# Eleven, nine and eight: where the 64-bit cosine weights are converted in an attention, experts and cosine-FFN kernel

## The chip, the cores and the metric

The kernel runs on one core of one Trainium2 chip. The time is the device time of one execution in microseconds (us). The engines of the core have names in the profile: PE is the matrix engine (PEld is its weight load), DVE the vector engine, ACT the scalar engine, POOL the GpSimd engine, and SP the engine whose queue issues nearly all DMAs here.

## The reference

```python
x = _attn_ref(q, k, v)            # 4 batches, 8 heads, 576 tokens, window 128 -> 2304 x 512
# experts: 8 of them, D = 512, F = 1024, tokens weighed by a Sinkhorn-normalised gate P
h = np.maximum(x @ w1[e], 0.0)
out += P[:, e:e + 1] * (h @ w2[e])
# cosine FFN: w_in 512 x 2048, w_out 2048 x 512, both float64 on the way in
h = x @ w_in
g = h * np.cos(h)
return (g @ w_out).astype(np.float32)
```

The two FFN weights come as 64-bit floats. The kernel reads them as pairs of 32-bit integers and makes 32-bit floats out of them on the chip.

## The kernel before

After the attention (about the first 195 us), the 2304 tokens are handled in three blocks of 768, first three expert blocks ("moe" 0, 1 and 2), then three FFN blocks. A block of experts is 32 units (8 experts, 4 slices of 256 hidden columns each, `u` from 0 to 31), an FFN block is 8 units. Each product of a unit is done with seven half-size products (a Strassen scheme, `m` in the order 5, 1, 4, 2, 3, 6, 7), and each operand is split into a high and a low part, so that one such product is six matmuls. All instructions are issued in an order that the program writes out by hand; each engine works through its own list in that order and waits where an operand isn't ready.

In block 0 a unit is the seven first-layer products (`product`, L938) and, between m = 6 and m = 7, `batch()`: six token tiles of the second layer (`g2`, L1163 to L1165), each followed by `evac` on DVE (L1154), with three PSUM banks gT[0..2] in turn. Beside it block 0 prepares its expert weights: `prep_a` splits the first-layer weights of the next unit (L142 on ACT, L145 on DVE: three instructions, the last one of 1024 columns), `prep_s` makes sums on POOL (L132), `prep_b` and `prep_sb` do the same for the second layer (L159, L184 on ACT, L161, L181 on POOL, L186 on DVE). The first product of a unit (m = 5, bank z) takes its weights from the part that the last L145 writes: `unit_mm` issues for each half high-high, high-low and low-high, so the third matmul of the product is the first to read the low part.

In blocks 1 and 2 the split weights are read back from DRAM (`load_a`, L115), the second layer runs as Strassen products too (`s_step`, L1077 on PE, evacuated by L1089 on DVE, operands from L1097 on DVE, L1101 on ACT, L1110 on POOL, weights by L1105 on SP's queue), and `load_p` brings a row of gate weights (L878).

Small work is woven in by generators. `slot()` steps the first one of each of the lists `pre`, `sbq`, `feed`, `bg` and `bg2` by one yield. In block 0 a unit calls it ten times: after the products 5, 1, 4, 2 and 7, and in `batch()` after each of the tiles 1 to 5, where `step_all(pre)` follows once more. In blocks 1 and 2 there are twelve calls in a unit. `bg` holds first the late gates, the Sinkhorn iterations and `p_rows` (its last act is the DMA at L866), and then `convert_f64`.

`convert_f64(c)` converts one chunk of 128 x 512 values. There are 32 chunks. Its steps, one for each call of `slot()`: DVE L260, ACT L264, nothing, DVE L267, DVE L271, DVE L275, DVE L279, the load of the next chunk (`load_f64`, L245 or L251 on SP's queue, 512 KB), nothing, the store of the result (L287, 256 KB). Four chunks are converted during the attention. When the chunks of an FFN unit are done, `prep_ffn` (in `bg2`) splits them: four sums on POOL (L132), eleven copies on ACT (L220), eleven differences on POOL (L222) and eleven stores (L216).

The lines that append a conversion are in the main loop, at the end of a unit:

```python
if chunk < 4 * NU2 and not bg and kind == "moe" and (b == 1 and u < NU1 - 6 or b == 2 and 0 < u < NU1 - 8) and u % 8 in (0, 2, 3, 5, 7):
    bg.append(convert_f64(chunk))
    chunk += 1
if b and ready < NU2 and 4 * (ready + 1) <= chunk - 1 + (not bg) and not bg2:
    bg2.append(prep_ffn(NU1 + ready))
    ready += 1
```

Of the kernel before, what the change touches and what calls it, by code (L numbers as in the profile page):

```python
# [29 lines left out]
def tile_attention_moe_cos_ffn(ctx, tc, q, k, v, w_gate, w1, w2, w_in, w_out, out):  # L30
# [9 lines left out]
    NU1 = E * UPE  # L40
    NU2 = DFF // FU
# [30 lines left out]
    with tc.manual_schedule():  # L72
# [38 lines left out]
        def load_a(u, ms):  # L111
            o = sorted(WI[m] for m in ms)
            o = slice(o[0], o[-1] + 1, o[-1] - o[0] or 1)
            out = waX[:, u % 2].bitcast(F32).rearrange("p (o w) -> p o w", o=7)
            nc.sync.dma_start(out=out[:, o], in_=wd1[u].rearrange("p (o w) -> p o w", o=7)[:, o])  # L115
# [187 lines left out]
        def stages(b, src):  # L303
            b11, b12, b21, b22 = quarters(b, src)
            st = {}
            stg[b] = st

            def stage(nm, i, x, y, over=None):
                if over:
                    t = st[over]  # L310
                elif b[0] == "ffn":
                    t = rawp.tile([P, 4, P, 2], F32, tag=("ra", "rb")[i], name=f"st{nm}_{b[0]}{b[1]}")
                    t = t.rearrange("p a f c -> p (a f c)")[:, :TB].rearrange("p (k f) -> p k f", k=2)
                else:
                    t = u_pool.tile([P, 2, HB], F32, tag=("u1", "u2")[i], name=f"st{nm}_{b[0]}{b[1]}")
                t = like(b, t) if not over else t
                nc.gpsimd.tensor_tensor(out=t, in0=x, in1=y, op=ALU.subtract)
                st[nm] = t

            stage("T1", 0, b12, b11)  # L320
            yield
            yield
            stage("T2", 1, b22, st["T1"])
            yield
            if b[0] == "ffn":
                yield
                stage("T3", 0, b22, b12)
                yield
                yield
                stage("T4", 1, b21, st["T2"])  # L330
                yield
            else:
                st["after"] = {"T2": lambda: stage("T4", 1, b21, st["T2"], "T2"),
                               "T1": lambda: stage("T3", 0, b22, b12, "T1")}
# [28 lines left out]
        def gate_block(j, pool, sb):  # L363
            b, o = j // 2, j % 2 * HB
            ps = pool[0].tile([P, 512], F32, tag=pool[1], name=f"gate{j}")
            for kc in range(KC):
                nc.tensor.matmul(ps[32 * kc:32 * kc + 32, :HB], wg[:, kc, :], xr[b][:, kc, o:o + HB],
                                 tile_position=(0, 32 * kc), skip_group_check=True)
            lT = sb if isinstance(sb, bass.AP) else sb.tile([P, HB], F32, tag="lT", name=f"lT{j}")
            nc.scalar.activation(out=lT, in_=ps[:, :HB], func=AF.Copy)  # L370
            return lT

        def gate_block2(j, lT, pool):
            ps = pool[0].tile([P, 512], F32, tag=pool[1], name=f"gateT{j}")
            for tt in range(GPB):
                nc.tensor.matmul(ps[:, tt * E:(tt + 1) * E], lT[:, tt * P:(tt + 1) * P], sel)
            nc.vector.tensor_copy(
                logits[:, j * GPB:(j + 1) * GPB, :].rearrange("p t e -> p (t e)"), ps[:, :GPB * E]
            )
# [334 lines left out]
        chunk = []  # L714
# [122 lines left out]
        bg, bg2, pre, feed, sbq = [], [], [], [], []  # L837

        def step_all(lst):
            if lst and next(lst[0], StopIteration) is StopIteration:  # L840
                lst.pop(0)

        def lazy(f):
            yield from f()
# [28 lines left out]
        def load_p(g):  # L873
            b, e = divmod(g, E)
            if b >= NB - 1:
                return
            src = pT.rearrange("(i e) t -> e i t", e=E)[e, b * TPB:(b + 1) * TPB, :]
            nc.sync.dma_start(out=Pb(g).rearrange("p (i t) -> p i t", t=P), in_=src.partition_broadcast(P))  # L878
# [335 lines left out]
        def tick():  # L1214
            tail[:] = [t for t in tail if next(t, StopIteration) is not StopIteration]

        def late_gates():
            bank_ = (LastBank(), "m")
            for j in range(next_half, 2 * NB):
                o = (1 + 2 * (j % 2)) * TB  # L1220
                lT = gate_block(j, bank_, cX[:, o:o + HB])
                yield
                yield
                gate_block2(j, lT, bank_)

        bg.append(late_gates())
        bg.append(sinkhorn((LastBank(), "m"), skp))
        bg.append(p_rows())
# [3 lines left out]
        chunk, ready = n_f64[0], 0  # L1232
# [17 lines left out]
        for n, s in enumerate(steps):  # L1250
            kind, b, u = s
            pre += pre_next
            pre_next.clear()
            ph = phases.index((kind, b))
            last = n + 1 == len(steps) or steps[n + 1][:2] != (kind, b)
            nxt = phases[ph + 1] if ph + 1 < len(phases) else None
            to_end = (NU1 if kind == "moe" else NU1 + NU2) - u
            if nxt and to_end == 4:
                if nxt[0] == "ffn":
                    feed.append(lazy(lambda nxt=nxt: stages(nxt, accs["moe", nxt[1]])))  # L1260
                else:
                    feed.append(stages(nxt, xr[nxt[1]]))
            if (kind, b, u) == ("moe", 1, 0):
                load_p(0)
            pace = NEXT if nx else {}
            if last and nxt:
                while feed:
                    step_all(feed)
                pace = LAST
                nx = combos(nxt, xr[nxt[1]] if nxt[0] == "moe" else accs["moe", nxt[1]])  # L1270
            lag = 1 if kind == "moe" else 2
            for m in (5, 1, 4, 2, 3, 6, 0, 7):
                if m == 0:
                    if queue and queue[0] <= n - lag:
                        while any(steps[queue[0]] == o for o in chained):
                            tick()
                        part = {0: range(GPB), 1: range(GPB, TPB)}[u] if (kind, b) == ("moe", 1) else range(TPB)
                        if n + 1 == len(steps):
                            part = range(GPB)
                        batch(tiles=part)  # L1280
                    while later:
                        later.pop(0)()
                    continue
                new = (kind, b) > ("moe", 0) or sigma[0] < 2 * NK and kind == "ffn"
                if m == 4:
                    if n:
                        product(steps[n - 1], 4)
                    begin(n + 1)
                else:
                    product(s, m)  # L1290
                while fetch:
                    load_a(*fetch.pop(0))
                if m in AHEAD:
                    d, ms = AHEAD[m]
                    if n + d < len(steps) and steps[n + d][:2] != ("moe", 0):
                        fetch.append((steps[n + d][2], ms))
                tick()
                if new:
                    couple()
                    if kind == "ffn" and (u > NU1 or m in (2, 3, 6, 7)) and sigma[0] < 2 * NK:  # L1300
                        s_step()
                    tick()
                    slot()
                if m not in (3, 6):
                    slot()
                elif (kind, b) == ("moe", 0) and u < UPE:
                    step_all(bg)
                for _ in range(pace.get(m, 0)):
                    next(nx, None)
            if pace is NEXT:  # L1310
                nx = None
            if kind == "ffn" or not b:
                queue.append(n)
            elif u % UPE == 0:
                load_p((b - 1) * E + u // UPE + 1)
            if chunk < 4 * NU2 and not bg and kind == "moe" and (b == 1 and u < NU1 - 6 or b == 2 and 0 < u < NU1 - 8) and u % 8 in (0, 2, 3, 5, 7):
                bg.append(convert_f64(chunk))
                chunk += 1
            if b and ready < NU2 and 4 * (ready + 1) <= chunk - 1 + (not bg) and not bg2:
                bg2.append(prep_ffn(NU1 + ready))  # L1320
                ready += 1
            while pre:
                step_all(pre)
            assert (kind, b, u) != ("moe", 2, NU1 - 5) or ready == NU2 and not bg2
# [41 lines left out]
```

## Time and profile before

| what | value |
|---|---|
| time, median of 3 runs | 1997.51 us (1997.01 to 1997.73) |
| span of the profiled execution | 1998.7 us |
| busy share of the span, PE | 98% |
| busy share of the span, DVE | 80% |
| busy share of the span, POOL | 46% |
| busy share of the span, ACT | 43% |
| instructions | 30931 |

The profile is of one execution. Its span, from the first to the last instruction, is 1.2 us above the median of the three timed runs, so nothing has to be added to the span. A row of the timeline reads: start, length (both in us from the span's start), engine, line, operation, what it writes and reads, shape, how many instructions were merged, and in brackets how long the engine had been idle before and what ended that. A row of the stages gives, for each engine, busy time and number of instructions in that stretch, then the granted clock of PE, the DMA share and GB/s. A row of one line's view gives the shortest, median and longest duration in ns.

### The profile page before, as it was taken

How to read it: one execution, taken by the hardware profiler on the slowest of the kernel's cores; microseconds unless marked ns; L12 is line 12 of the kernel's file. 1: busy time of each engine (PE TensorE's matmuls, PEld its weight loads, DVE VectorE, ACT ScalarE, POOL GpSimd, SP SyncE). 2: the span in 40 equal slices, each digit the busy share in tenths (PEclk: the TensorE clock that was granted, in tenths of full speed). 3: DMA queues.
4: the chain of work that ended last, by engine and by line, in shares of the span. 5: the costliest groups of instructions: out<-in, count | busy, mean ns of one | idle time of the engine just before them, and what ended most of it. 6: DMA issues, size and time to landing. Idle time of an engine off the chain costs nothing.

```text
span 1998.7 us, 30931 instructions
## 1 busy us (share of the span) xinstructions
PE 1962.6 (98%) x10970; PEld 1822.9 (91%) x10970; DVE 1594.0 (80%) x2670; ACT 862.0 (43%) x1616; POOL 916.6 (46%) x777
## 2 busy tenths in 40 slices
PE   8999999999999999999999999999999999999999
PEld 5667899999999999999999999999999999998998
DVE  7785877777777789989988978899987886757766
ACT  6895444444444333333333433333333354544543
POOL 4673566666566434443436522444353413333221
PEclk9999999999999999999999999999999999999999
DMA  7754788888888898998999788889898765565552
GB/s 199 211 139 151 259 312 293 312 303 313 304 298 307 312 334 311 336 330 313 340 322 329 257 285 291 319 322 333 318 328 285 250 218 176 202 227 180 205 186 99
DMA packets 293754, 540.04 MB, mean 270 GB/s; under 512 B 80256, under 2 KB 141792, under 8 KB 286432
## 3 DMA queue, kind: packets, MB, share of 16 engines
q1 hardware_dynamic: 293056, 537.94, 77.6%
q8 instruction: 87, 1.43, 0.3%
q14 instruction: 67, 0.55, 0.1%
q10 hardware_dynamic: 544, 0.13, 0.0%
HBM read 384.32 MB, written 153.67 MB: 269 GB/s over the span
## 4 chain that ended last, share of the span: by engine, by line
PE 83%; DVE 6%; DMA 2%; ACT 1%; issue 1%; POOL 0%; ACTq 0%; DVEq 0%; POOLq 0%
PE gT L1077 21%; PE y_moe L938 18%; PE z_moe L938 9%; PE gT L1165 7%; PE gT L1164 7%; PE gT L1163 7%; PE y_ffn L938 5%; PE x_moe L938 4%; PE z_ffn L938 2%; DMA wbX<-wdp 2%; DVE hX L1097 1%; PE x_ffn L938 1%; DVE acc_moe L1089 1%; DVE waX L145 0%; DVE fb L271 0%
## 5 line engine op out<-in xcount | busy, mean ns | idle before, releaser
L1077 PE MATMUL gT<-hX,wbX 128*128 128x384 f32 x2688 | 540.4, 335 | 8.6 <-DMA wbX<-wdp 3.5
L1077 PEld LDWEIGHTS gT<-hX,wbX 128*128 128x128 f32 x2688 | 470.9, 188 | 15.1 <-DVE acc_moe L1089 5.6
L938 PE MATMUL y_moe<-xtT_moe,waX 128*128 128x384 f32 x1728 | 347.1, 335 | 0.6 <-ACT s_moe L967 0.6
L938 PEld LDWEIGHTS y_moe<-xtT_moe,waX 128*128 128x128 f32 x1728 | 304.5, 188 | 3.6 <-ACT s_moe L967 0.9
L1089 DVE TENSOR_TENSOR acc_moe<-gT,acc_moe 128x384 f32<-128x384 f32 x432 | 236.8, 549 | 65.9 <-PE gT L1077 64.7
L1163 PE MATMUL gT<-wbX,hX 128*128 128x512 f32 x660 | 257.6, 390 | 1.3 <-DVE acc_moe L1154 1.3
L1165 PE MATMUL gT<-wbX,hX 128*128 128x512 f32 x660 | 258.0, 391 | 0.0
L1164 PE MATMUL gT<-wbX,hX 128*128 128x512 f32 x660 | 257.8, 391 | 0.0
L967 ACT ACTIVATE s_moe<-y_moe 128x384 f32<-128x384 f32 x192 | 93.3, 486 | 344.1 <-PE y_moe L938 344.1
L1110 POOL TENSOR_TENSOR hodd<-hodd 128x768 f32<-128x768 f32 x64 | 132.5, 2070 | 167.4 <-DVE hX L1097 81.5
L1110 POOL TENSOR_TENSOR cX<-cX 128x768 f32<-128x768 f32 x64 | 126.4, 1975 | 173.0 <-DVE hX L1097 94.7
L927 POOL TENSOR_TENSOR hX<-cX,hX 128x768 fp32r<-128x768 f32 x44 | 84.5, 1936 | 251.7 <-ACT hX L924 210.8
L132 POOL TENSOR_TENSOR s<-ra 128x256 f32<-128x256 f32 x80 | 62.4, 780 | 254.4 <-DVE waX L145 179.0
L1154 DVE SCALAR_TENSOR_TENSOR acc_moe<-gT,prob,acc_moe 128x512 f32<-128x512 f32 x174 | 129.6, 747 | 37.8 <-PE gT L1165 35.8
L1163 PEld LDWEIGHTS gT<-wbX,hX 128*128 128x128 f32 x660 | 123.9, 188 | 26.4 <-DVE acc_moe L1154 2.1
L1097 DVE TENSOR_TENSOR hX<-cX,hX 128x768 fp32r<-128x768 f32 x112 | 147.0, 1313 | 0.9 <-ACT hX L1101 0.9
L1165 PEld LDWEIGHTS gT<-wbX,hX 128*128 128x128 f32 x660 | 123.8, 188 | 26.0
L1164 PEld LDWEIGHTS gT<-wbX,hX 128*128 128x128 f32 x660 | 123.9, 188 | 24.6
L1097 DVE TENSOR_TENSOR hX<-hodd,hX 128x768 fp32r<-128x768 f32 x112 | 141.3, 1262 | 0.0
L883 ACT ACTIVATE hX<-cX 128x768 fp32r<-128x768 f32 x64 | 43.9, 686 | 219.9 <-DVE cX L970 219.9
L938 PE MATMUL z_moe<-xtT_moe,waX 128*128 128x384 f32 x576 | 116.2, 335 | 1.7 <-DVE hodd L970 1.3
L938 PE MATMUL z_moe<-xtB_moe,waX 128*128 128x384 f32 x576 | 115.9, 335 | 0.0
(206 smaller groups left out, 3765.5 us busy)
## 6 DMA issues: line engine op xcount, KB each, us to landing
waX<-wd SPq DMA_DIRECT2D x264, 512.0 KB, 5.6
wbX<-wdp SPq DMA_DIRECT2D x224, 512.0 KB, 6.7
wd<-waX SPq DMA_DIRECT2D x32, 1792.0 KB, 6.8
wdp<-sb SPq DMA_DIRECT2D x32, 1024.0 KB, 6.2
wdp<-wbX SPq DMA_DIRECT2D x96, 256.0 KB, 4.4
wbX<-wd SPq DMA_DIRECT2D x24, 1024.0 KB, 4.9
waX<-wd SPq DMA_DIRECT2D x88, 256.0 KB, 5.2
ra<-in_moe_w_dram SPq DMA_DIRECT2D x64, 256.0 KB, 7.4
```

Of the source, the lines that this page charges most:

```text
L132: nc.gpsimd.tensor_tensor(out=s4[:, o], in0=x, in1=y, op=op)
L927: eng.tensor_tensor(out=h[:, 1], in0=c, in1=h[:, 0].bitcast(F32), op=ALU.subtract)
L938: nc.tensor.matmul(ps[:, :HB], wa[:, WI[m], wl, kc, :], x[:, xl, kc, :], start=start and kc == 0 and n_ == 0, stop=stop and kc == 1 and n_ ...
L967: nc.scalar.activation(out=t["s", i], in_=ps[:, :HB], func=AF.Copy)
L1077: nc.tensor.matmul(ps[:, :HB], w[:, u, wl, d * P:(d + 1) * P], x[:, xl, u, :], start=m in (1, 5, 2) and n_ == 0, stop=m in (4, 3, 2) and n ...
L1089: nc.vector.tensor_tensor(out=a, in0=ps[:, :HB], in1=a, op=ALU.add)
L1097: nc.vector.tensor_tensor(out=x[:, 1], in0=H[:, q], in1=x[:, 0].bitcast(F32), op=ALU.subtract)
L1110: nc.gpsimd.tensor_tensor(out=H[:, t[0]], in0=H[:, t[1]], in1=H[:, t[2]], op=ALU.subtract)
L1154: nc.vector.scalar_tensor_tensor(out=a, in0=ps, scalar=pe, in1=a, op0=ALU.mult, op1=ALU.add)
L1163: nc.tensor.matmul(ps, hf[f][:, 0, ts], wb[:, f, 0, :], start=f == 0, stop=False)
L1164: nc.tensor.matmul(ps, hf[f][:, 0, ts], wb[:, f, 1, :], start=False, stop=False)
L1165: nc.tensor.matmul(ps, hf[f][:, 1, ts], wb[:, f, 0, :], start=False, stop=f == 1)
```

## The change

The condition under which a conversion is appended at the end of a unit is replaced by a table of units for each block. In block 0 a conversion is appended at the end of the units 5, 7, ... 25 (11), in block 1 at 0, 3, ... 24 (9), in block 2 at 1, 3, ... 15 (8). Before, it was none in block 0, 16 in block 1 (units with u % 8 in 0, 2, 3, 5, 7 below 26) and 12 in block 2. The four during the attention stay.

```diff
+        F64_AT = (range(5, 26, 2), range(0, 26, 3), range(1, 16, 2))
         bg.append(late_gates())
@@
-            if chunk < 4 * NU2 and not bg and kind == "moe" and (b == 1 and u < NU1 - 6 or b == 2 and 0 < u < NU1 - 8) and u % 8 in (0, 2, 3, 5, 7):
+            if chunk < 4 * NU2 and not bg and kind == "moe" and u in F64_AT[b]:
                 bg.append(convert_f64(chunk))
                 chunk += 1
```

## Rows read from the trace of the kernel before

**Rows 1.** Busy time by stage: middle of block 0, then blocks 1 and 2.
```profile
250.00:640.00 390.00, 390.00 (x1962) 353.45 (x1961) 300.45 (x403) 170.57 (x276) 254.49 (x230) 1.00 0.85 304
695.00:1127.00 432.00, 427.96 (x2464) 424.83 (x2462) 382.10 (x549) 155.03 (x273) 194.20 (x130) 1.00 0.91 325
1127.00:1617.00 490.00, 484.10 (x2773) 480.09 (x2774) 423.30 (x609) 164.59 (x277) 195.77 (x119) 1.00 0.85 298
```

**Rows 2.** Waits of PE's weight loads, 695 to 1620 us: total, times, longest.
```profile
PEld gT L1077 <- DVE acc_moe L1089: 5.6, 10, 1.0
PEld gT L1077 <- DMA wbX<-wdp: 4.4, 3, 2.0
```

**Rows 3.** SP's issue of the last act of the Sinkhorn work, by its line.
```profile
L866 SPq DMA_DIRECT2D pT<-logits x1: 346/346/346, 228.8 to 228.8; - x1
```

**Rows 4.** A conversion's instructions by line, 695 to 1620 us: shortest, median, longest.
```profile
L264 ACT ACTIVATE fa<-fa,ebias x27: 722/725/729, 699.0 to 1430.1; 128x512 int32<-128x512 int32 x27
L267 DVE SCALAR_TENSOR_TENSOR fa<-f,fa x27: 676/691/1471, 699.8 to 1431.3; 128x512 int32<-128x512 int32 x27
L271 DVE TENSOR_SCALAR fb<-f x27: 408/417/2064, 704.9 to 1432.8; 128x512 int32<-128x512 int32 x27
L275 DVE SCALAR_TENSOR_TENSOR fb<-f,fb x27: 692/693/1114, 705.9 to 1433.3; 128x512 f32<-128x512 uint32 x27
L279 DVE SCALAR_TENSOR_TENSOR fb<-fb,fa x27: 674/682/689, 707.4 to 1435.7; 128x512 f32<-128x512 f32 x27
```

**Rows 5.** Timeline of DVE in one unit of block 0.
```profile
399.04 1.66 DVE L186 TENSOR_TENSOR sb<-sb 128x1024 fp32r<-128x1024 f32 x1 [0.71 <-ACT sb L184]
...
401.21 0.55 DVE L970 TENSOR_TENSOR cX<-x_moe,s_moe 128x384 f32<-128x384 f32 x1
402.73 0.56 DVE L970 TENSOR_TENSOR cX<-z_moe,s_moe 128x384 f32<-128x384 f32 x1 [0.97 <-ACT s_moe L967]
...
406.27 0.75 DVE L1154 SCALAR_TENSOR_TENSOR acc_moe<-gT,prob,acc_moe 128x512 f32<-128x512 f32 x1 [0.43 <-PE gT L1165]
407.63 0.75 DVE L1154 SCALAR_TENSOR_TENSOR acc_moe<-gT,prob,acc_moe 128x512 f32<-128x512 f32 x1 [0.61 <-PE gT L1165]
408.30 0.68 DVE L145 TENSOR_TENSOR waX<-ra,waX 128x512 fp32r<-128x512 f32 x1
...
409.66 0.41 DVE L145 TENSOR_TENSOR waX<-ra,waX 128x256 fp32r<-128x256 f32 x1
409.99 1.22 DVE L145 TENSOR_TENSOR waX<-s,waX 128x1024 fp32r<-128x1024 f32 x1
```

**Rows 6.** Timeline of POOL in the same unit.
```profile
397.86 1.06 POOL L132 TENSOR_TENSOR s<-s,ra 128x256 f32<-128x256 f32 x1
...
401.26 2.40 POOL L161 TENSOR_TENSOR wbX<-rb,wbX 128x1024 fp32r<-128x1024 f32 x1
...
411.29 0.73 POOL L132 TENSOR_TENSOR s<-ra 128x256 f32<-128x256 f32 x1 [5.50 <-DVE waX L145]
```

**Rows 7.** Timeline of PE: the next unit's first two products.
```profile
411.21 1.20 PE L938 MATMUL z_moe<-xtT_moe,waX 128*128 128x384 f32 x6
412.25 1.20 PE L938 MATMUL y_moe<-xtB_moe,waX 128*128 128x384 f32 x6
```

**Rows 8.** Timeline of block 1: a conversion's L267 beside POOL's L1110.
```profile
1028.43 1.90 POOL L1110 TENSOR_TENSOR hodd<-hodd 128x768 f32<-128x768 f32 x1 [1.89 <-DVE hX L1097]
...
1029.42 1.46 DVE L267 SCALAR_TENSOR_TENSOR fa<-f,fa 128x512 int32<-128x512 int32 x1 [0.33 <-ACT fa L264]
```

**Rows 9.** Timeline of an early unit of block 0, with Sinkhorn work on DVE.
```profile
205.19 1.22 DVE L145 TENSOR_TENSOR waX<-s,waX 128x1024 fp32r<-128x1024 f32 x1
...
205.71 0.51 PE L938 MATMUL z_moe<-xtT_moe,waX 128*128 128x384 f32 x2
...
206.46 0.98 PE L938 MATMUL z_moe<-xtT_moe,waX 128*128 128x384 f32 x4 [0.24 <-DVE waX L145]
...
207.28 1.21 PE L938 MATMUL y_moe<-xtB_moe,waX 128*128 128x384 f32 x6
```

## Prediction

> **What bounds the kernel now.** I read the stages first. In the middle of block 0 PE is busy for the whole 390 us, at a granted clock of 1.00 (the 2.4 GHz level) [rows 1]. Nothing can be gained there, because there is no idle PE time to take away; something can be lost. In blocks 1 and 2 PE is idle for 432 - 428.0 = 4.0 us and 490 - 484.1 = 5.9 us [rows 1], the changes of block at either end included. So what the change can win lies in blocks 1 and 2 and is small. The second view, the waits of PE's weight loads in that stretch, tells whose it is: 5.6 us in ten waits for DVE's evacuation L1089, 4.4 us in three waits for a weight DMA [rows 2]. A conversion is DVE work, so it bears on the 5.6 us first. The third view is the timeline of one unit of block 0, DVE, POOL and PE beside each other [rows 5 to 7]. It decides the case: it shows how much room DVE has at the places where the conversion's steps will fall, and who waits for DVE next.
>
> **What is added in block 0.** The Sinkhorn work in `bg` has ended at 228.8 us [rows 3], in the third or fourth unit, so the list is empty at unit 5 and eleven conversions run, each in the unit after the one that appended it (ten calls of `slot()`, one unit; a unit has 78 matmuls, so 1962 of them in 390 us [rows 1] make 15.5 us a unit). By the order of the calls, L260 follows product 5 and stands just ahead of L186 (399.04), L264 goes behind ACT's work after product 1, L267 follows the L970 that starts at 401.21, and L271, L275 and L279 follow the evacuations of tiles 1, 2 and 3. L279 stands ahead of the first L145 (408.30). I lay the conversion over the unit of rows 5 to 7.
>
> L260 meets POOL's L132 (397.86 to 398.92), ends about 0.3 behind it and is nearly swallowed by the 0.71 us that DVE waits ahead of L186; it pushes POOL's next instructions by about 0.2, so L161 runs from 401.46 to 403.86 in place of 401.26 to 403.66 [rows 5, 6]. L264 takes 0.72 us of ACT [rows 4] ahead of what DVE awaits next, so the L970 of 401.21 comes at about 401.9 and L267 can start at about 402.3.
>
> Here is the main term. L267 takes 0.69 us in most cases, but up to 1.47 [rows 4]. The long ones are those that start while a POOL instruction is under way: at 1029.42 L267 started 0.99 us into an L1110 that ended at 1030.33, and ended itself at 1030.88, 0.55 behind it [rows 8]. A start inside a POOL instruction waits for its end and then takes 0.55. In block 0 L267 falls inside L161 in every unit, since 402.3 lies between 401.46 and 403.86. So it ends at 403.86 + 0.55 = 404.41, and the L970 that now starts at 402.73 starts at 404.33: 1.60 late. The 0.97 us that DVE idles ahead of it now [rows 5] has gone into this.
>
> The Trainium skill says the same of the cause (SBUF — State Buffer, section Who interferes with whom): a vector instruction with two SBUF inputs and a GpSimd instruction that reads SBUF exclude each other, and whoever started first keeps the shared ports for its whole length. It would put the block-0 term at the collision price below, 19.6 us, and a plain sharing of bandwidth would put it nearer the free price, 4.2 us; the trace agrees with the rule [rows 8].
>
> From there on DVE is back to back. Consecutive DVE instructions start about 0.08 ahead of the end of the one before (409.66 + 0.41 against 409.99 [rows 5]), so L271, L275 and L279 cost 0.42, 0.69 and 0.68 less 0.08 each, 1.55 in all [rows 4]; POOL has nothing to do until L145 has ended (idle 5.50 us before 411.29 [rows 6]), so these three meet no POOL instruction. Against them stand the idle times ahead of the evacuations of tiles 2 and 3, 0.43 and 0.61, with the overlap 0.51 and 0.69 [rows 5]. So the first L145, and the chain of three behind it, which has no idle time in it now, comes 1.60 + 1.55 - 1.20 = 1.95 late. The last L145 now ends at 409.99 + 1.22 = 411.21, just when the next unit's first product starts [rows 5, 7]. It would end at about 413.16.
>
> What that costs is seen where Sinkhorn work stood in the same place: L145 ended at 206.41, 0.70 after the product's start at 205.71; the first two matmuls ran, the other four waited until 206.46, and the next product began at 207.28, 1.57 after the start in place of 412.25 - 411.21 = 1.04 [rows 7, 9]. So 0.70 of lateness cost 0.53, the first 0.17 being free. 1.95 costs 1.78 us. PE shifts by as much, the next unit has no conversion and DVE's idle times to recover in, so nothing carries over: 11 x 1.78 = 19.6 us.
>
> Bounds for this term: below, if L267 found POOL free, it would be 0.61 behind 402.3, the L970 0.2 late, the sum 0.2 + 0.35 = 0.55, less 0.17 = 0.38, times eleven 4.2 us. Less than nothing is excluded, since PE is never idle there [rows 1]. Above: the evacuation of tile 1 would end at about 407.4, just when tile 4 takes the same PSUM bank; 0.3 us more for each gives 23 us. I take 19.6, since the row that is nearest, L267 inside a POOL instruction, is the case here.
>
> The eleven loads and stores (768 KB each time) are hidden: in SP's queue they stand behind L275 and L279, which are done by then, and the block's own loads are two units ahead. At 304 GB/s [rows 1] eleven take about 28 us of DMA time in some 340 us, so the share rises from 0.85 to about 0.92, which is what block 1 has now. If that cover is gone, a late load costs what one does in block 1, up to 2.0 us [rows 2].
>
> **What is taken from blocks 1 and 2.** 28 conversions become 17. The 5.6 us of waits for the evacuation [rows 2] are where L275 and L279 stand ahead of it; by share 5.6 x 11 / 28 = 2.2 us go. Bounds: all of it (5.6) and nothing. The earlier chunks also let `prep_ffn` start without waiting for a conversion, one start more in block 1, one fewer in block 2: its POOL and DMA work is the same in sum, and moves. Its raw loads would fall on a `load_p` more often, and a weight DMA that comes late behind them costs up to 2.0 us [rows 2]; I take 0 and keep 4 us for the range.
>
> **Sum.** Against the profiled span: 1998.7 + 19.6 - 2.2 = 2016.1. The span stands 1.2 us above the median of the runs, so the forecast for the median is 1997.5 + 17.4 = 2014.9 us, 0.9% slower.
>
> **Rivals.** (a) L267 does not sit inside L161 (POOL later or earlier by a few tenths than I place it): the free price, 1997.5 + 4.2 - 2.2 = 1999.5. For it: the row is laid by hand, and it is a matter of 1.5 us; against it: L161 is 2.40 long and L267 lies 0.9 behind its start. (b) Faster: DVE's idle time, (390 - 300.45) x 15.5 / 390 = 3.6 us a unit [rows 1], takes up the whole conversion, the last L145 ends less than 0.17 late (the point from which PE waits), block 0 costs nothing, and the ten waits for L1089 in blocks 1 and 2 vanish: 1997.5 - 5.6 = 1991.9. Against it: even the free price is over that point. (c) Block 0 as forecast, and the moved `prep_ffn` starts meet the `load_p` in two more places: 2014.9 + 4 = 2019, and with the bank of tile 4 late too 2022. (d) The change doesn't do what it says, if `bg` were not empty in time: each conversion that slides to a later unit leaves 1.8 us out; its last act is over at 228.8 [rows 3].
>
> **How the numbers follow.** The forecast (2009 to 2018) 0.66, (a) 0.13, (b) 0.10, (c) 0.10, (d) 0.01. 0.2% is 4 us, about what a measurement can tell from no change. Slower by more are the forecast and (c), 0.76; within it (a), (d) and a part of (b) where little is won, 0.15; faster 0.09. The range goes from (a) to (c): 1999 to 2021, which leaves (b) and the end of (c) out.
>
> **What would show it.** In the profile after: PE's idle time between 250 and 640 us, nothing now, some 18 us, in eleven waits of about 1.7 us for DVE L145, every second unit; L267 in block 0 some 2.1 us long, ending 0.55 behind L161; the last L145 of those units 17.3 us behind the one before, in place of 15.5. In blocks 1 and 2 fewer waits for L1089. If L267 shows 0.69 there, (a) holds and the step with L161 is wrong; if L145 comes late and PE doesn't wait, the step with the third matmul is wrong; if PE's idle time grows in blocks 1 and 2, it is the moved preparations.

## The result and the profile after

The changed kernel takes 2014.07 us (median of 4 runs, 2011.57 to 2015.43), the kernel before 1997.26 us beside it: a ratio of 1.0081, 95% interval 1.0068 to 1.0093. It is slower by 0.8%, and the forecast was 2014.9 us. In a later comparison with both kernels run again it was 2011.58 against 1997.71 us, 1.0070 (1.0054 to 1.0087).

First the stages of the profile after; the columns are those of [rows 1]. The middle of block 0 is the same stretch, blocks 1 and 2 come some 18 us later.

```profile
250.00:640.00 390.00, 377.51 (x1874) 336.42 (x1873) 333.84 (x440) 169.74 (x276) 242.85 (x219) 1.00 0.89 313
...
713.00:1145.00 432.00, 429.84 (x2482) 428.08 (x2481) 366.82 (x518) 151.84 (x269) 190.33 (x135) 1.00 0.92 317
1145.00:1635.00 490.00, 484.61 (x2772) 481.16 (x2771) 410.28 (x588) 162.53 (x273) 192.01 (x116) 1.00 0.85 287
```

Against [rows 1], PE does 1874 matmuls in the 390 us of block 0 in place of 1962. 88 missing matmuls at 78 a unit of 15.5 us are 17.5 us. The granted clock is 1.00 as before. PE's idle time in the row, 12.5 us, understates the loss, since the modelled end of a pipelined matmul reaches into the wait behind it; the count doesn't.

The next rows tell whom PE and its weight loads wait for in block 0, where before neither waited for anybody. A row gives engine and line, what it waits for, total, times, longest.

```profile
PE z_moe L938 <- DVE waX L145: 12.5, 11, 1.2
...
PEld gT L1163 <- DVE acc_moe L1154: 3.2, 11, 0.3
```

There are eleven waits for eleven conversions. One of them follows in three views of one unit. DVE:

```profile
262.26 2.11 DVE L267 SCALAR_TENSOR_TENSOR fa<-f,fa 128x512 int32<-128x512 int32 x1
264.29 0.55 DVE L970 TENSOR_TENSOR cX<-z_moe,s_moe 128x384 f32<-128x384 f32 x1
...
267.29 0.42 DVE L271 TENSOR_SCALAR fb<-f 128x512 int32<-128x512 int32 x1
...
269.54 0.69 DVE L279 SCALAR_TENSOR_TENSOR fb<-fb,fa 128x512 f32<-128x512 f32 x1
...
271.73 1.23 DVE L145 TENSOR_TENSOR waX<-s,waX 128x1024 fp32r<-128x1024 f32 x1
```

POOL:

```profile
261.42 2.40 POOL L161 TENSOR_TENSOR wbX<-rb,wbX 128x1024 fp32r<-128x1024 f32 x1
```

PE:

```profile
271.39 0.51 PE L938 MATMUL z_moe<-xtT_moe,waX 128*128 128x384 f32 x2
273.01 0.96 PE L938 MATMUL z_moe<-xtT_moe,waX 128*128 128x384 f32 x4 [1.11 <-DVE waX L145]
273.81 1.22 PE L938 MATMUL y_moe<-xtB_moe,waX 128*128 128x384 f32 x6
```

L267 starts 0.84 into L161, which ends at 263.82, and ends at 264.37, 0.55 behind it: 2.11 us for an instruction that takes 0.69 alone. From there DVE is late until the last L145 ends at 272.96. PE issues two matmuls of the product and stands until 273.01, and the next product starts 2.42 after this one in place of 1.04 [rows 7]. In all eleven, L267 takes 2.11 to 2.12 us and ends 0.55 behind L161.

The whole change by stretches, each from the start of the second product of the unit named (found in PE's timeline by counting the matmuls of L938), from profiled executions of the two kernels, twice each:

| stretch, us | before | before, again | after | after, again |
|---|---|---|---|---|
| block 0, unit 5 to 27 | 341.15 | 341.15 | 358.91 | 358.70 |
| block 0, unit 27, to block 1, unit 0 | 79.42 | 79.44 | 79.45 | 79.46 |
| block 1, unit 1 to 30 | 425.50 | 424.60 | 422.34 | 421.99 |
| turn, unit 30 of block 1 to unit 1 of block 2 | 46.80 | 46.79 | 49.54 | 47.95 |
| block 2, unit 1 to 30 | 426.85 | 426.48 | 424.89 | 423.38 |
| the rest of block 2, and the FFN blocks | 425.85 | 425.89 | 425.86 | 425.85 |

### The profile page after: what moved, and what is told of

The parts are those of the page before. It is cut to its first block, busy times and chain, and to the rows that moved or that the text cites. A ratio compares the mean times of both kernels' runs of the same rounds, so it can differ in the third digit from the quotient of the medians.

```text
span 2013.6 us, 30936 instructions
## 1 busy us (share of the span) xinstructions
PE 1970.4 (98%) x10970; PEld 1825.4 (91%) x10970; DVE 1610.6 (80%) x2670; ACT 862.4 (43%) x1616; POOL 908.2 (45%) x777
## 4 chain that ended last, share of the span: by engine, by line
PE 68%; DVE 9%; POOL 7%; DMA 5%; issue 2%; SPq 1%; ACT 0%; POOLq 0%; DVEq 0%; ACTq 0%
PE gT L1077 21%; PE y_moe L938 14%; PE z_moe L938 7%; PE y_ffn L938 5%; PE gT L1165 4%; PE gT L1164 4%; PE gT L1163 4%; PE x_moe L938 3%; POOL s L132 3%; DVE waX L145 3%; POOL wbX L161 2%; DMA wdp<-wbX 2%; PE z_ffn L938 2%; DMA rb<-in_moe_w_dram 2%; POOL sb L181 2%
## 5 line engine op out<-in xcount | busy, mean ns | idle before, releaser
L938 PE MATMUL y_moe<-xtT_moe,waX 128*128 128x384 f32 x1728 | 347.2, 335 | 0.6 <-ACT s_moe L967 0.6
L938 PEld LDWEIGHTS y_moe<-xtT_moe,waX 128*128 128x128 f32 x1728 | 304.7, 188 | 3.6 <-ACT s_moe L967 0.9
L1089 DVE TENSOR_TENSOR acc_moe<-gT,acc_moe 128x384 f32<-128x384 f32 x432 | 237.1, 551 | 84.4 <-PE gT L1077 83.6
L1110 POOL TENSOR_TENSOR hodd<-hodd 128x768 f32<-128x768 f32 x64 | 124.4, 1944 | 190.3 <-DVE hX L1097 96.4
L1110 POOL TENSOR_TENSOR cX<-cX 128x768 f32<-128x768 f32 x64 | 125.7, 1963 | 183.5 <-DVE hX L1097 100.3
L132 POOL TENSOR_TENSOR s<-ra 128x256 f32<-128x256 f32 x80 | 65.3, 816 | 264.7 <-DVE waX L145 190.9
L1097 DVE TENSOR_TENSOR hX<-cX,hX 128x768 fp32r<-128x768 f32 x112 | 148.5, 1326 | 0.5 <-ACT hX L1101 0.5
L1154 DVE SCALAR_TENSOR_TENSOR acc_moe<-gT,prob,acc_moe 128x512 f32<-128x512 f32 x174 | 129.6, 747 | 21.5 <-PE gT L1165 19.7
L1097 DVE TENSOR_TENSOR hX<-hodd,hX 128x768 fp32r<-128x768 f32 x112 | 145.2, 1296 | 0.0
L938 PE MATMUL z_moe<-xtT_moe,waX 128*128 128x384 f32 x576 | 119.3, 337 | 13.6 <-DVE waX L145 12.7
L938 PEld LDWEIGHTS z_moe<-xtT_moe,waX 128*128 128x128 f32 x576 | 100.7, 188 | 18.2 <-DVE waX L145 17.0
```

The source lines that it names most:

```text
L132: nc.gpsimd.tensor_tensor(out=s4[:, o], in0=x, in1=y, op=op)
L938: nc.tensor.matmul(ps[:, :HB], wa[:, WI[m], wl, kc, :], x[:, xl, kc, :], start=start and kc == 0 and n_ == 0, stop=stop and kc == 1 and n_ ...
L1089: nc.vector.tensor_tensor(out=a, in0=ps[:, :HB], in1=a, op=ALU.add)
L1097: nc.vector.tensor_tensor(out=x[:, 1], in0=H[:, q], in1=x[:, 0].bitcast(F32), op=ALU.subtract)
L1110: nc.gpsimd.tensor_tensor(out=H[:, t[0]], in0=H[:, t[1]], in1=H[:, t[2]], op=ALU.subtract)
L1154: nc.vector.scalar_tensor_tensor(out=a, in0=ps, scalar=pe, in1=a, op0=ALU.mult, op1=ALU.add)
```

## The experiments

**Block 0 alone.** The kernel before, with eleven conversions repeated in block 0.

```diff
...
+            if kind == "moe" and not b and not bg and u in range(5, 26, 2):
+                bg.append(again_f64())   # L260 to L279 on the chunk that is there, no load, no store
             if chunk < 4 * NU2 and not bg and kind == "moe" and (b == 1 and u < NU1 - 6 or ...
```

> The kernel before, with eleven conversions repeated in block 0 (units 5, 7, ... 25): the five DVE and one ACT instructions of one chunk that is already there, with no load and no store, and the result is not used. Blocks 1 and 2 keep their 28. If DVE's lateness is what costs (L267 caught inside POOL's L161, the last L145 late, PE's third matmul waiting), block 0 grows by the 17.8 us seen in the changed kernel and the time is 1997.3 + 17.8 = 2015 us. If it is the DMA traffic of the moved conversions, nothing of it is here, and the time stays at 1997 us. If half is each, 2006. What the run has over the changed kernel is then what blocks 1 and 2 gave back, 2 to 3 us.

2016.06 us, 1.0095 (1.0080 to 1.0110) of the kernel before. Block 0 from unit 5 to 27 takes 358.77 us in place of 341.15, 17.6 us more, with the same waits as in the changed kernel. Its row of the stages and its row of PE's waits:

```profile
250.00:640.00 390.00, 377.39 (x1875) 336.49 (x1874) 333.60 (x440) 169.60 (x275) 242.57 (x218) 1.00 0.82 292
```

```profile
PE z_moe L938 <- DVE waX L145: 12.6, 11, 1.2
```

No DMA belongs to these conversions (the DMA share is 0.82, below the 0.85 of [rows 1]), and the price is the same to 0.2 us. So the loss is block 0's, and the moved transfers have no part in it. What blocks 1 and 2 give back can't be read from this run: with their 28 conversions they took 896.7 us here, as long as with 17 in the changed kernel's first profile. That is taken up below.

**An operand in PSUM.** The changed kernel; only the place of one tile differs in block 0.

```diff
-            a = u_pool.tile([P, 512], I32, tag="u1", name=f"fa{c}")
+            a = u_pool.tile([P, 512], I32, tag="u1", name=f"fa{c}") if bank is None else bank.bitcast(I32)
...
-                bg.append(convert_f64(chunk))
+                bg.append(convert_f64(chunk, None if b else gT[3]))
```

> The changed kernel; in block 0 the tile fa of a conversion lies in the PSUM bank gT[3], which is free there, in place of SBUF. The same instructions in the same order at the same places; L267 has one SBUF input and one from PSUM. If the price comes from L267 waiting for a POOL instruction under way because both of its inputs are in SBUF, L267 takes about 0.7 us in place of 2.1, the last L145 is some 0.5 us late in place of 1.8, PE loses about 0.4 us for each, and the time is 2014.1 - 17.8 + 4.2 = 2000.5 us. If it is the work itself on a busy DVE, wherever the operand lies, or the DMA traffic, the time stays at 2014 us.

1998.26 us, 1.0003 (0.9993 to 1.0012) of the kernel before, 2.2 us less than expected. Block 0 from unit 5 to 27: 344.66 us, 3.5 more than before in place of 17.8. Its DVE, its POOL and its stage:

```profile
262.33 0.69 DVE L267 SCALAR_TENSOR_TENSOR gT<-f,gT 128x512 int32<-128x512 int32 x1
```

```profile
261.35 2.41 POOL L161 TENSOR_TENSOR wbX<-rb,wbX 128x1024 fp32r<-128x1024 f32 x1
```

```profile
250.00:640.00 390.00, 389.60 (x1946) 350.17 (x1945) 328.54 (x455) 174.82 (x285) 252.15 (x227) 1.00 0.91 323
```

L267 starts 0.98 into L161, as in the changed kernel, and takes 0.69: the wait is gone with one of its two SBUF inputs, while its place, its work and the DMAs are the same. L260, which now writes to PSUM, takes 0.68 us in all eleven, beside the same L132, in place of 0.96 in the changed kernel. The rest of the lateness, what L271, L275 and L279 add, stays and costs 3.5 us / 11 = 0.32 for each conversion; the prediction's lower bound had 0.38.

**Other places.** The changed kernel; in block 0 the same steps fall on other calls of `slot()`.

```diff
+            if spread:
+                yield          # L267 one call later: after the evacuation of tile 1
             nc.vector.scalar_tensor_tensor(out=a, in0=hi, ...)          # L267
             ...                                                          # L271
+            if spread:
+                yield          # L275 after tile 5, L279 after product 7
+                yield
...
             load_f64(c + 1)
             yield
-            yield
+            if not spread:
+                yield
...
-                bg.append(convert_f64(chunk))
+                bg.append(convert_f64(chunk, not b))
```

By the calls, the load of the next chunk comes three calls later than in the changed kernel and the store two, both in the next unit, not one call each as the expectation has it.

> The changed kernel; in block 0 the steps of a conversion fall on other calls: L267 after the evacuation of tile 1, L271 after that of tile 2, L275 after tile 5 (behind the last L145), L279 after product 7, the load of the next chunk and the store one call each later. All the work of the eleven conversions stays in block 0. If the place is what costs, L267 meets an idle POOL (0.69 us), L267 and L271 fit into the idle 0.43 and 0.61 us, the last L145 is not late, and block 0 costs nothing: 2014.1 - 17.8 = 1996.3 us. If DVE's load in block 0 costs by itself, or the DMAs, the time stays at 2014 us; if only the wait for L161 goes and the rest of the lateness stays, 2000.5.

1995.24 us, 0.9988 (0.9978 to 0.9997) of the kernel before. Block 0 from unit 5 to 27: 341.15 us, as before, with all eleven conversions in it. PE waits for nobody there. Its stage, then DVE in one unit (the lines of this kernel are a few numbers higher: L269 is L267, L273 is L271, L284 is L279), then POOL and PE:

```profile
250.00:640.00 390.00, 390.00 (x1962) 353.44 (x1961) 340.84 (x458) 175.67 (x287) 267.05 (x230) 1.00 0.92 326
```

```profile
265.61 0.68 DVE L269 SCALAR_TENSOR_TENSOR fa<-f,fa 128x512 int32<-128x512 int32 x1
...
266.87 0.41 DVE L273 TENSOR_SCALAR fb<-f 128x512 int32<-128x512 int32 x1
...
269.65 1.22 DVE L145 TENSOR_TENSOR waX<-s,waX 128x1024 fp32r<-128x1024 f32 x1
...
273.87 1.23 DVE L284 SCALAR_TENSOR_TENSOR fb<-fb,fa 128x512 f32<-128x512 f32 x1
```

```profile
273.49 1.06 POOL L132 TENSOR_TENSOR s<-s,ra 128x256 f32<-128x256 f32 x1
```

```profile
270.88 1.20 PE L944 MATMUL z_moe<-xtT_moe,waX 128*128 128x384 f32 x6
```

The last L145 ends at 270.87, when the product starts, as it does in [rows 5, 7]. DVE's busy time rises to 340.8 of 390 us and the DMA share to 0.92, both above the changed kernel's, and PE loses nothing: neither load by itself is the cause. Nor is a wait for POOL by itself: L284 starts 0.38 us into L132, takes 1.23 us in place of 0.68 and ends 0.55 behind POOL, as L267 does in the changed kernel. But it stands behind the last L145, and PE doesn't feel it.

**The low part last.** The changed kernel; in block 0 the first product of a unit reads the low part of the weights with its fifth and sixth matmul, not with the third and sixth.

```diff
+            seq = [(kc, wl, xl) for kc in range(2) for wl, xl in ((0, 0), (0, 1), (1, 0))]
+            if (kind, b, m) == ("moe", 0, 5):
+                seq.sort(key=lambda t: t[1])
...
```

> The changed kernel; in block 0 the first product of a unit (m = 5) issues its six matmuls in another order: the four that read the high part of the weights first, then the two that read the low part, which the last L145 writes. If PE waits at the first matmul that reads the low part, two more matmuls (0.35 us) run ahead of the wait, each of the eleven waits is 0.35 us shorter, and the time is 2014.1 - 3.8 = 2010.3 us, block 0 from unit 5 to 27 355.1 us in place of 358.9. If PE waits for something else there (the bank, the whole tile of weights, the evacuations), the order changes nothing: 2014.

2009.56 us, 1.0059 (1.0046 to 1.0073) of the kernel before; block 0 from unit 5 to 27 takes 354.95 us. PE in one unit:

```profile
271.20 0.86 PE L940 MATMUL z_moe<-xtT_moe,waX 128*128 128x384 f32 x4
272.86 0.62 PE L940 MATMUL z_moe<-xtT_moe,waX 128*128 128x384 f32 x2 [0.80 <-DVE waX L145]
```

Now four matmuls run ahead of the wait, and each conversion costs (358.91 - 354.95) / 11 = 0.36 us less, the length of two matmuls. PE does wait at the first matmul that reads the low part, and there alone.

**No preparation across the turn.** The changed kernel; the sixth `prep_ffn` starts after the first unit of block 2.

```diff
-            if b and ready < NU2 and 4 * (ready + 1) <= chunk - 1 + (not bg) and not bg2:
+            if b and ready < NU2 and 4 * (ready + 1) <= chunk - 1 + (not bg) and not bg2 and not (b == 1 and u > 26):
```

> The changed kernel, but no preparation of an FFN unit starts after unit 26 of block 1: the one that starts at unit 30 in the changed kernel and runs across the turn from block 1 to block 2 starts after the first unit of block 2. In the changed kernel the stretch from unit 30 of block 1 to unit 1 of block 2 is 49.5 us in place of 46.8. If that preparation's POOL, ACT and DMA work is what lengthens the turn, it is 46.8 again and the time is 2014.1 - 2.7 = 2011.4 us, less what the third preparation costs in block 2 (0 to 2 us). If the turn is longer for another reason (the conversions gone from ahead of it), it stays 49.5 and the time 2014.

2010.89 us, 1.0068 (1.0051 to 1.0085). The turn takes 46.65 us in place of 49.54. POOL there, first in the changed kernel:

```profile
1133.47 1.45 POOL L132 TENSOR_TENSOR s<-ra 128x256 f32<-128x256 f32 x1
...
1138.50 1.45 POOL L132 TENSOR_TENSOR s<-s,ra 128x256 f32<-128x256 f32 x1
1139.92 1.44 POOL L132 TENSOR_TENSOR s<-ra 128x256 f32<-128x256 f32 x1
```

and here:

```profile
1134.56 2.57 POOL L350 TENSOR_TENSOR xtB_moe<-xr,xtB_moe 128x768 fp32r<-128x768 f32 x1
1137.09 1.85 POOL L1110 TENSOR_TENSOR cX<-cX 128x768 f32<-128x768 f32 x1
1138.90 2.56 POOL L350 TENSOR_TENSOR xtB_moe<-xr,xtB_moe 128x768 fp32r<-128x768 f32 x1
```

The sums of the preparation are gone from between the operands of the next block. In the profile that gives the turn its old length. The preparation's ACT work and its stores went away from the turn with the sums, so the run shows the price of the preparation, not that of its POOL work alone. In time, 2010.89 us is less than the changed kernel's medians (2011.58 and 2014.07 in two comparisons), but the interval overlaps with both of theirs, so a gain of 3 us in the timed runs isn't shown by this run alone.

**Both cures.** The other places, and no preparation across the turn.

> The changed kernel with both cures: the other places in block 0 and no preparation across the turn from block 1 to block 2. If the two causes are apart from each other, the gains add: 1995.2 us (places) less the 3.2 us that the other run took off, 1992 us, and 0.2 to 0.3% less than the kernel before. If the preparation merely moves its cost elsewhere when block 0 is undisturbed, 1995.

1993.09 us, 0.9980 (0.9971 to 0.9989) of the kernel before: 2.1 us less than with the other places alone, where 3.2 were expected. The two gains add up within what can be told, and the result is 0.2% faster than the kernel before and faster than the changed one. The stretch from unit 5 to 27 of block 0 is 341.15 us, the turn 46.68, and blocks 1 and 2 with the turn take 891.1 us.

**Both kernels again.** What one profile of blocks 1 and 2 is worth.

> The kernel before, profiled a second time, to see how much one profile of blocks 1 and 2 differs from the next. If the 2.4 us that blocks 1 and 2 are shorter in the changed kernel come from the conversions that left them, the stretch from unit 1 of block 1 to unit 30 of block 2 is 899 us again (425.5 + 46.8 + 426.9) and the weight loads wait about 5.6 us for L1089. If it is scatter of the weight DMAs, the stretch can be 897 us here too, with the waits for L1089 unchanged and fewer waits for the DMA.

> The changed kernel, profiled a second time beside it. Block 0 from unit 5 to 27 is 358.9 us again, since the eleven waits repeat to 0.1 us. In blocks 1 and 2: 896.8 us again (422.3 + 49.5 + 424.9) with 1.6 us of waits for L1089 if the gain belongs to the change, anything from 896 to 900 if it is scatter.

The kernel before took 1997.98 us, 0.9997 (0.9988 to 1.0007) of the runs beside it, the changed one 2011.58, as said above. Their stretches stand in the table: block 0 repeats to 0.2 us, blocks 1 and 2 don't. From unit 1 of block 1 to unit 30 of block 2 the changed kernel takes 893.3 us this time, less than either case of the expectation had (896.8, or 896 to 900).

The waits of PE's weight loads in blocks 1 and 2, first the kernel before again, then the changed one again:

```profile
PEld gT L1077 <- DVE acc_moe L1089: 5.0, 9, 0.9
PEld gT L1077 <- DVE hX L1097: 3.9, 6, 1.4
PEld gT L1077 <- DMA wbX<-wdp: 3.8, 3, 1.4
```

```profile
PEld gT L1077 <- DVE hX L1097: 6.6, 9, 1.4
PEld gT L1077 <- DVE acc_moe L1089: 1.3, 4, 0.5
...
PEld gT L1077 <- DMA wbX<-wdp: 0.5, 1, 0.5
```

With 28 conversions the waits for L1089 are 5.6 [rows 2], 5.0 here and 4.9 us in the block-0 run; with 17 they are 1.6, 1.3, and 0.8 and 1.7 in the PSUM and the places run. That is the change's doing. The waits for L1097 go the other way, 3.9 to 4.1 against 6.1 to 6.6; with the preparation off the turn they are 5.2, and what makes the rest no run shows. The waits for the weight DMA scatter: 4.4, 3.8 and 2.5 with 28, 2.2, 0.5, 0.5 and 1.3 with 17. From unit 1 of block 1 to unit 30 of block 2 the three profiles with 28 take 899.2, 897.9 and 896.7 us, the five with 17 and the preparation at the turn 896.8, 893.3, 892.4, 895.8 and 895.1 (the last is the low-part run): 897.9 against 894.7 on the mean, so some 3 us are won, with a scatter of 2 us either way from one execution to the next.

## Why the prediction was right, step by step

- **Where it can be won or lost** held. PE had no idle time in block 0, and all of the loss is there; blocks 1 and 2 gave back some 3 us.
- **The place of each step** held: L260 ahead of L186, L267 inside L161, L271, L275 and L279 ahead of the first L145. The L145 ahead of the unit shown ends at 272.96 - 17.28 = 255.68, that ahead of the unit of [rows 5, 6] at 411.21 - 15.50 = 395.71, which is 140.03 us later, so L267 was expected at 262.3 and started at 262.26.
- **L267 inside L161** held to the digit: 0.55 behind POOL's end, as in [rows 8]. The PSUM run shows the cause, not only the coincidence: with one input outside SBUF the same instruction beside the same L161 takes 0.69. The rule of the Trainium skill that the prediction weighed (SBUF — State Buffer, Who interferes with whom) agrees with both rows. Rival (a), which had L267 free, is what the PSUM run costs: 3.5 us in block 0 against its 4.2.
- **The lateness of the last L145** was 1.95 in the sum and is 17.28 - 15.50 = 1.78 in the profile (17.28 us lie between the last L145 of this unit and of the one ahead of it, in place of one unit's 15.50). The mechanism was right and a size was off by 0.17 us. The L970 behind L267 came where it was laid (264.29 against 264.30 on this unit's scale). The term that was too large is the chain of three L145, taken to move as a whole: from the start of the first (270.14) to the end of the last it takes 2.82 us in place of 411.21 - 408.30 = 2.91 [rows 5], since its first step closes up too when DVE is back to back; the other 0.08 are hundredths in the steps ahead of it.
- **The third matmul** held: 1.57 us of lateness against the product's start cost 2.42 - 1.04 = 1.38, so 0.19 was free (0.17 in the sum), and the order of the six matmuls moves the price by two of them. The bank of tile 4, kept for the upper bound only, was late as feared: PE's weight loads wait 3.2 us for L1154 in eleven times, and of the 17.76 / 11 = 1.61 us that a conversion costs, 1.61 - 1.38 = 0.23 pass there, ahead of the product. But this doesn't come on top, as the bound of 23 us had it. DVE has no idle time between 266.63 and the end of the last L145, so nothing that PE does there moves that end, and the third matmul waits for it whether the bank was late or not: 1.78 - 0.17 = 1.61 is the whole price already.
- **The sum for block 0** was 19.6 and is 17.8 us, and the 0.17 us of the lateness, eleven times, are the difference.
- **Blocks 1 and 2** were to give back 2.2 us and give some 3 by the profiles. The shift behind it was mis-sized in its parts: the waits for L1089 lost some 4 us, not 2.2, the waits for L1097 gained 2.5, and the sixth preparation at the turn costs 1.2 to 2.7 us, which the sum had at nothing and as a DMA's price at most. What the timeline shows at the turn is its POOL work among the next block's operands; that this, and not its ACT work or its stores, lengthens the turn is likely but not shown.
- **Luck.** That the time came out within 0.8 us of 2014.9 is in part luck. Both errors go the same way: by the stretches the change costs 17.8 us and gives back some 3, less than 15 us in all, where the sum had 17.4. The two comparisons of times gave 16.8 and 13.9 us.
- **The span** was taken as the time. Later profiles show the time of the same execution beside its span (2015.43 against 2013.6 for the changed kernel, 1998.78 against 1997.0 for the kernel before): 1.8 us lie around it. Both kernels have them, so the difference is not touched.
- Of the rivals, (b) fell with the first wait in block 0, (c)'s mechanism, DMAs at the moved starts, doesn't show (fewer DMA waits, not more), and (d) fell with the eleven L267.

## What to carry to other kernels

DVE at 77% has room on the mean, but a conversion, some 2.9 us of DVE work where nothing holds it up (0.41 for L260, and 0.69, 0.42, 0.69 and 0.68 [rows 4]), is paid or free by its place: the same eleven conversions cost 17.8 us, 3.5 us (with one operand in PSUM) or nothing in what were 341 us. Before work is woven into a loop that has no idle PE time, lay each of its instructions on the timeline of one turn, and look for two things: which instruction of the other engine is under way when it starts, and which operand it delays that PE reads first in the next turn. Here an instruction with both inputs in SBUF shouldn't start inside a long POOL instruction if what stands behind it has no slack; one input in PSUM, or a later call, took the wait away. One input alone is no protection: L260 reads one SBUF tile and writes SBUF, and in all eleven units of the changed kernel it starts inside L132 and ends 0.28 us behind it.

## What the runs showed of the hardware

A DVE instruction that waits for POOL counts as busy: L267 shows 2.11 us beside L161 with both inputs in SBUF and 0.69 with one of them in PSUM, and the stage of block 0 has 333.8 us of busy DVE in the changed kernel and 328.5 in the PSUM run, though the latter gets through more units. A busy share is therefore no measure of work where the two engines meet. And PE needs the low part of its weights only at the matmul that names it: the two matmuls ahead of the wait ran, and four ran when the order allowed it, which took 0.36 us off the price of each conversion.
